# The 128 output rows that a fused retention and MoE kernel computes last, cut as 384 and 128 columns, with the last store issued from ScalarE

## Chip, cores, metric

One core of a Trainium2 chip. The metric is the device time of one execution in microseconds; the "span" is the stretch from the first to the last instruction in a profile, some 1.8 us shorter than that time in the executions of this study that give both. By its time and granted clock (the share of TensorE's full clock that the profiler shows as granted) the record labels each execution fast or slow.

## The reference

Retention (attention with a decay instead of a softmax) over 8 batches, 8 heads, 576 positions and 64 channels, and then a two-layer network with a quick GELU on the 4608 rows:

```python
def _attn_ref(q, k, v):                       # cut
    scores = scale * np.matmul(q, k.transpose(0, 1, 3, 2))
    ret = scores * Dmat[None, :, :, :]        # Dmat: decay, zero above the diagonal
    return np.matmul(ret, v).astype(np.float32)

def _moe_ref(x, w_in, w_out):                 # x: (4608, 512)
    h = x @ w_in                              # w_in: (512, 2048)
    g = h * (1.0 / (1.0 + np.exp(-1.702 * h)))
    return (g @ w_out).astype(np.float32)     # w_out: (2048, 512)
```

Only the last piece of `g @ w_out` to be computed matters below: 128 rows of the output, 512 columns each.

## The kernel before: the parts concerned

The output is made in 36 units of 128 rows. For each unit, `down` multiplies 16 slices of 128 features into one bank of PSUM, the memory that receives TensorE's sums, and `down_out` copies the bank to SBUF, the on-chip working memory (there `osb`), and stores it to the output in DRAM. The helper `op` puts an operation into an engine's stream and derives the waits from what it reads and writes. At the end SyncE waits for the last stores.

```python
def down(c, r, s, b, n0=0, n1=DM):
    for f in range(4 * s, 4 * s + 4):
        op("pe", lambda e, f=f: e.matmul(
            bank[b][:, 0 : n1 - n0], gT[c % 2][:, f, P * r : P * r + P], w_out_sb[:, f, n0:n1],
            start=(f == 0), stop=(f == NF - 1)), ...)

def down_out(c, r, b, n0=0, n1=DM, cp="act"):
    ...
    src, dst = bank[b][:, 0 : n1 - n0], osb[i][:, n0:n1]
    if cp == "act":
        op("act", lambda e: e.activation(dst, src, AF.Copy), ...)
    else:
        op("dve", lambda e: e.tensor_copy(dst, src), ...)
    ...                                        # f issues the store, one DMA per block of rows
    return op("sp", f, reads=[f"osb{i}_{n0}"], ...)

# last chunk of four units, in steady()
if c == NCH - 1:
    for r in (3, 0, 1):
        ...                                    # whole units: 16 matmuls of 512 columns, copy, store
    for n0, b, cp in ((0, "B", "act"), (256, "A", "dve")):
        for s in range(4):
            down(c, 2, s, b, n0, n0 + 256)
        finish_unit(c, 2, b, n0=n0, n1=n0 + 256, cp=cp)
    break
```

So the last unit is already cut in two halves of 256 columns: ScalarE copies the first half while TensorE multiplies the second, and VectorE copies the second.

## Time and profile before

| | before |
|---|---|
| time, median of the first 3 executions | 296.37 us (296.10 to 296.77) |
| span of the profile | 295.1 us |
| TensorE busy | 96% of the span |
| last unit: first matmul to the end of the span | 288.78 to 295.09 us |
| of it, after the last matmul's result | 2.6 us: copy 0.42, store 1.67, closing 0.48, gaps |

The views are read from the whole to the end: first which engine the chain of waits runs through (TensorE), then the timeline of the last 5 us, then the one store that ends last. The prediction shows these lines. "Landing" is the moment when a store's completion is seen, and "closing" is what follows the last landing.

### The profile page before, as it was taken

The numbers are of one execution on the slowest core, as the hardware profiler recorded it, in microseconds if no ns is written. First come the engines' busy times: TensorE is split into PE (matmuls) and PEld (weight loads), VectorE is DVE, ScalarE is ACT, GpSimd is POOL, SyncE is SP. The second block draws the span as 40 slices with busy tenths as digits, with TensorE's granted clock in tenths as the row PEclk, the third lists the DMA queues.
The fourth block names the chain that finished last, engine by engine and source line by source line (L and its number), as shares of the span: only waits on it lengthen the run. The fifth ranks groups of instructions, "written<-read, shape, count | busy, mean of one in ns | idle before, by whom it ended". The sixth has DMA issues, their size and how long they took to land.

```text
span 295.1 us, 8029 instructions
## 1 busy us (share of the span) xinstructions
PE 284.5 (96%) x3620; PEld 142.1 (48%) x3651; DVE 99.6 (34%) x202; ACT 134.0 (45%) x235; POOL 110.1 (37%) x141
## 2 busy tenths in 40 slices
PE   5899999999999999999999999999999999999996
PEld 5567355884533453345434543454344434443344
DVE  5672037534571543034503470237014700410000
ACT  7456433662356225622573246424642365216511
POOL 9999797000970680292039202920080000000000
PEclk9799999999999999999999999999999999999999
DMA  9999999997999999499369925991691050110021
GB/s 169 182 214 205 205 223 252 243 107 176 166 232 117 123 209 207 97 162 197 107 121 144 203 83 131 168 194 63 153 136 66 26 134 2 38 71 38 0 71 71
DMA packets 116786, 40.63 MB, mean 138 GB/s; under 512 B 104080, under 2 KB 109968, under 8 KB 116752
## 3 DMA queue, kind: packets, MB, share of 16 engines
q0 software_dynamic: 79712, 22.82, 67.5%
q1 hardware_dynamic: 37040, 17.31, 23.3%
q8 instruction: 28, 0.46, 0.6%
q14 instruction: 6, 0.05, 0.1%
HBM read 36.70 MB, written 9.44 MB: 156 GB/s over the span
## 4 chain that ended last, share of the span: by engine, by line
PE 95%; DMA 2%; issue 2%; DVE 1%; ACT 0%; SPq 0%
PE psA L582 21%; PE psB L582 20%; PE psA L556 18%; PE psB L556 17%; PE psB L570 4%; PE psA L570 3%; PE psX L481 2%; DMA osb<-in_q_dram 2%; PE psC L497 1%; PE psY L519 1%; PE psX L519 1%; PE psA L674 1%; PE psK L426 1%; PE psE L426 1%; PE psD L497 1%
## 5 line engine op out<-in xcount | busy, mean ns | idle before, releaser
L226 POOL DMA_DIRECT2D kqn<-in_k_dram x39 | 35.2, 913 | 109.0 <-DMA kqT<-kqn 107.3
L582 PE MATMUL psA<-w_out_sb,gT 128*128 128x512 bf16 (+1 forms) x287 | 66.8, 373 | 2.4 <-issue 2.2
L582 PE MATMUL psB<-w_out_sb,gT 128*128 128x512 bf16 (+1 forms) x285 | 63.9, 373 | 0.5 <-issue 0.5
L556 PE MATMUL psB<-xT,w_in_sb 128*128 128x512 bf16 x233 | 61.2, 379 | 0.4
L556 PE MATMUL psA<-xT,w_in_sb 128*128 128x512 bf16 x239 | 61.4, 379 | 0.1
L544 DVE TENSOR_TENSOR xT<-psX,gq 128x512 bf16<-128x512 f32 x16 | 11.1, 691 | 113.4 <-PE psX L519 113.4
L450 ACT ACTIVATE kv<-stm 128x1024 bf16<-128x1024 f32 (+1 forms) x18 | 15.6, 866 | 68.5 <-DVE stm L441 68.5
L582 PEld LDWEIGHTS psB<-w_out_sb,gT 128*128 128x128 bf16 x288 | 27.8, 98 | 31.8 <-ACT gT L561 0.3
L582 PEld LDWEIGHTS psA<-w_out_sb,gT 128*128 128x128 bf16 x304 | 27.8, 98 | 31.7 <-ACT gT L561 2.5
L561 ACT ACTIVATE gT<-psB 128x512 bf16<-128x512 f32 x60 | 35.8, 597 | 15.8 <-PE psB L556 15.7
L561 ACT ACTIVATE gT<-psA 128x512 bf16<-128x512 f32 x60 | 35.8, 597 | 15.6 <-PE psA L556 15.6
L239 POOL DMA_DIRECT2D vn<-in_v_dram x40 | 37.3, 947 | 0.1
L556 PEld LDWEIGHTS psA<-xT,w_in_sb 128*128 128x128 bf16 x240 | 19.1, 97 | 32.6 <-ACT gT L561 16.6
L556 PEld LDWEIGHTS psB<-xT,w_in_sb 128*128 128x128 bf16 x240 | 18.8, 97 | 33.0 <-ACT gT L561 16.3
L226 POOL DMA_DIRECT2D kqn<-in_q_dram x37 | 33.6, 921 | 0.3 <-issue 0.3
L345 DVE TENSOR_TENSOR vp<-vn,vfac 128x512 bf16<-128x512 f32 x36 | 23.2, 684 | 24.0 <-DMA vn<-in_v_dram 24.0
L592 ACT ACTIVATE osb<-psB 128x512 f32<-128x512 f32 (+1 forms) x18 | 10.5, 585 | 21.6 <-PE psB L582 21.6
L592 ACT ACTIVATE osb<-psA 128x512 f32<-128x512 f32 x18 | 10.5, 584 | 15.3 <-PE psA L582 15.3
L506 DVE TENSOR_TENSOR pm<-psC,mask 128x512 bf16<-128x512 f32 (+1 forms) x20 | 12.6, 629 | 8.8 <-PE psD L497 8.7
L506 DVE TENSOR_TENSOR pm<-psD,mask 128x512 bf16<-128x512 f32 (+1 forms) x20 | 12.5, 626 | 0.0
L570 PE MATMUL psB<-xT,w_in_sb 128*128 128x256 bf16 (+1 forms) x104 | 12.5, 265 | 0.0
L441 DVE TENSOR_TENSOR stm<-psE,stm 128x256 f32<-128x256 f32 x28 | 11.9, 424 | 1.2
(86 smaller groups left out, 257.9 us busy)
## 6 DMA issues: line engine op xcount, KB each, us to landing
vn<-in_v_dram POOLq DMA_DIRECT2D x32, 256.0 KB, 5.7
out_dram<-osb SPq DMA_DIRECT2D x31, 256.0 KB, 2.2
kqn<-in_k_dram POOLq DMA_DIRECT2D x31, 128.0 KB, 5.4
kqn<-in_q_dram POOLq DMA_DIRECT2D x31, 128.0 KB, 5.4
w_out_sb<-in_moe_w_out_dram POOLq DMA_DIRECT2D x4, 512.0 KB, 13.4
out_dram<-osb SPq DMA_DIRECT2D x10, 128.0 KB, 2.4
w_in_sb<-in_moe_w_in_dram POOLq DMA_DIRECT2D x8, 128.0 KB, 5.4
w_in_sb<-in_moe_w_in_dram POOLq DMA_DIRECT2D x4, 256.0 KB, 7.5
```

The costliest lines, as they stand in the source:

```text
L226: e.dma_start(kqn[sl][p0 : p0 + n, which, :, :], src[b, :, s0 : s0 + n, :].rearrange("h p d -> p h d"),)
L239: e.dma_start(vn[sl][p0 : p0 + n, :, :], v[b, :, s0 : s0 + n, :].rearrange("h p d -> p h d"))
L345: op(eng, lambda e: e.tensor_tensor(vp[u % NVP].ap(), vn[sl].ap(), vfac[:, ty, :, None].to_broadcast([P, H, DH]), ALU.mult), reads=[f"vn{s ...
L441: op("dve", lambda e: e.tensor_tensor(dst, src, prev, ALU.add), reads=[KB[a], f"stm{(i - 1) % 8}"], writes=[f"stm{i % 8}"])
L450: op("act", lambda e: e.activation(kv[:, i0 % NKV : i0 % NKV + n, :, :], stm[:, i0 % 8 : i0 % 8 + n, :, :], AF.Copy), reads=[f"stm{(i0 + i ...
L506: op("dve", lambda e: e.tensor_tensor(pm[(u0 // 2) % 2][hh][:, c0:c1].rearrange("p (a i) -> p a i", i=64), ps32(SB[hh])[:, c0:c1].rearrang ...
L544: op("dve", lambda e: e.tensor_tensor(xT[ch % 2][:, slice(hh, 4, 2), P * jj : P * jj + 2 * P].rearrange("p g (u t) -> p u g t", u=2), ps32 ...
L556: op("pe", lambda e, a=a: e.matmul(bank[b][:, n0:n1], w_in_sb[:, a, P * f : P * f + P], xT[c % 2][:, a, n0:n1], start=(a == 0), stop=(a == ...
L561: op("act", lambda e: e.activation(gT[c % 2][:, f, n0:n1], bank[b][:, n0:n1], AF.Gelu_apprx_sigmoid), reads=[b], writes=[f"g{c % 2}_{f}_{j ...
L570: op("pe", lambda e, a=a, f=f, i=i: e.matmul(bank[b][:, n * i : n * i + n], w_in_sb[:, a, P * f : P * f + P], xT[c % 2][:, a, P * lo : P * ...
L582: op("pe", lambda e, f=f: e.matmul(bank[b][:, 0 : n1 - n0], gT[c % 2][:, f, P * r : P * r + P], w_out_sb[:, f, n0:n1], start=(f == 0), sto ...
L592: op("act", lambda e: e.activation(dst, src, AF.Copy), reads=[b], writes=[f"osb{i}_{n0}"])
```

## The change

The intent: keep TensorE's work as it is, but leave less to copy and to store after the last matmul. The first piece grows to 384 columns, the last shrinks to 128. The second part of the change issues the last store from ScalarE's queue, so that it need not stand behind the other store in SyncE's.

```diff
-        def down_out(c, r, b, n0=0, n1=DM, cp="act"):
+        def down_out(c, r, b, n0=0, n1=DM, cp="act", eng="sp"):
...
-            return op("sp", f, reads=[f"osb{i}_{n0}"], writes=[f"out{u}_{n0}"],
+            return op(eng, f, reads=[f"osb{i}_{n0}"], writes=[f"out{u}_{n0}"],
...
-                    for n0, b, cp in ((0, "B", "act"), (256, "A", "dve")):
+                    for n0, n1, b, cp in ((0, 384, "B", "act"), (384, 512, "A", "dve")):
                         for s in range(4):
-                            down(c, 2, s, b, n0, n0 + 256)
-                        finish_unit(c, 2, b, n0=n0, n1=n0 + 256, cp=cp)
+                            down(c, 2, s, b, n0, n1)
+                        finish_unit(c, 2, b, n0=n0, n1=n1, cp=cp, eng="sp" if n0 == 0 else "act")
```

## The prediction

> **What bounds the kernel now.** I read three views, from the whole to the last microseconds. First the page: busy time of the engines, and the chain that ended last.
>
> ```profile
> PE 284.5 (96%) x3620; PEld 142.1 (48%) x3651; DVE 99.6 (34%) x202; ACT 134.0 (45%) x235; POOL 110.1 (37%) x141
> ...
> PE 95%; DMA 2%; issue 2%; DVE 1%; ACT 0%; SPq 0%
> ```
>
> TensorE (PE) is busy for 96% of the 295.1 us span and makes up 95% of the chain. No line that the diff touches runs before the last 128-row block, the third unit of the last chunk. So 288.8 us are the same in both kernels, and only the end can move. The timeline from 290.4 us, with start and length ahead of each group:
>
> ```profile
> 290.53 1.91 PE L582 MATMUL psA<-w_out_sb,gT 128*128 128x256 bf16 x16
> 290.73 0.38 ACT L592 ACTIVATE osb<-psB 128x256 f32<-128x256 f32 x1 [1.15 <-PE psB L582]
> 291.14 2.12 SPq L598 DMA_DIRECT2D out_dram<-osb  x2
> 292.48 0.42 DVE L594 COPY osb<-psA 128x256 f32<-128x256 f32 x1 [32.51 <-PE psA L582]
> ```
>
> The second half block is multiplied until 292.44 us (290.53 + 1.91), copied out of PSUM by VectorE (DVE) until 292.90, and stored. That final store, asked for on its own by the window from 292.5 us:
>
> ```profile
> L598 SPq DMA_DIRECT2D out_dram<-osb x1: 332/332/332, 292.9 to 292.9; - x1
> ...
> DMA to landing us min/median/max: 1.7/1.7/1.7
> ```
>
> The reader is to see three steps in a row with nothing beside them: copy 0.42, store 1.7 from its issue at 292.93 to landing at about 294.60, and then 0.49 us of closing handshakes up to 295.09. What the store does in its 1.7 us shows in the sums over three stretches, whose last two columns are DMA share and GB/s:
>
> ```profile
> 293.20:293.76 0.56, 0.00 (x0) 0.00 (x0) 0.00 (x0) 0.00 (x0) 0.00 (x0) 1.00 0.00 0
> 293.76:294.26 0.50, 0.00 (x0) 0.00 (x0) 0.00 (x0) 0.00 (x0) 0.00 (x0) 1.00 0.75 262
> 294.26:294.60 0.34, 0.00 (x0) 0.00 (x0) 0.00 (x0) 0.00 (x0) 0.00 (x0) 1.00 0.00 0
> ```
>
> Of the 1.67 us about 0.83 pass before the first byte, 0.49 move data, and 0.35 pass until the completion is seen. Only the middle part can depend on the size.
>
> **What the Trainium skill says.** "DMA: Bandwidth & Descriptors", section "Issuing engines are not separate DMA queues", states that stores from the scalar and the sync engine end on the same 16 DMA engines, and that issuing from both saves only the sequencer's issue time. The issue here is 0.33 us. The trace can't confirm the ScalarE side: this kernel issues nothing from there. Its section "Anatomy of one DMA — SWDGE (gpsimd) path", written for the other kind of issue, calls most of a DMA's fixed cost a write receipt that doesn't scale with bytes; the 0.35 us of quiet after the last byte agrees in kind, though here it is the smaller part. "TensorE: Matmul & The Clock Gate", section "Back-to-back issue gap", gives a sustained 81 ns for matmuls with 128 columns and calls 56 ns the isolated gap. The trace decides for 56: two runs of sixteen such matmuls with fresh weights, in the timeline around 24.4 us,
>
> ```profile
> 24.65 1.06 PE L570 MATMUL psC<-xT,w_in_sb 128*128 128x128 bf16 x16
> 25.54 1.06 PE L570 MATMUL psB<-xT,w_in_sb 128*128 128x128 bf16 x16
> ```
>
> start 0.89 us apart, 55.6 ns each. "VectorE: DVE Perf Modes", section "Why PSUM operands drop a tier", says that a float32 copy out of PSUM runs at one element per cycle, so its time has a part that falls with the columns; the trace agrees below.
>
> **The change part by part.** The last block is cut as 384 + 128 columns, not 256 + 256, and the small last store is issued by ScalarE.
>
> *Matmuls.* Removed are 2 x 16 of 256 columns, added 16 of 384 and 16 of 128. The steps are 1.75 / 16 = 109 ns at 256 (the two groups of the before start at 288.78 and 290.53), 3.45 / 16 = 216 ns at 512, so 162.5 at 384 by interpolation, and 55.6 at 128. Sum before: 32 x 109 = 3.50 us. Sum after: 16 x 162.5 + 16 x 55.6 = 2.60 + 0.89 = 3.49 us. The last result is due when the last matmul ends: before 290.53 + 1.91 = 292.44. After, the small group starts at 288.78 + 2.60 = 291.38 and takes the 1.06 us of the row above: 292.44. TensorE's end doesn't move. All are on the path, and they cancel.
>
> *Copy of 384 columns, ScalarE.* 383 ns at 256 and 597 at 512, so 490 ns by interpolation. It starts when its matmuls end, 288.78 + 15 x 0.1625 + 0.33 = 291.55, and ends near 292.07, beside the small matmuls. Off the path, and ScalarE is free 0.7 us before it must issue the last store.
>
> *Store of 384 columns, SyncE queue.* Issued near 292.09. Its 192 KB lie between 128 KB (1.7 us) and 256 KB (2.0 us), so it lands in some 1.85 us, at 293.94; data flow from 292.92 to about 293.57. Off the path if the last store lands later.
>
> *Copy of 128 columns, VectorE.* This one is on the path. The copy of 256 took 424 ns; the VectorE rows that read PSUM go from 424 ns (256 columns) to about 685 (512), 1.02 ns for each column. 128 fewer columns save 0.13 us: 0.29 us, end near 292.77.
>
> *Last store, ScalarE queue.* Issue at 292.79 instead of 292.93. From 256 to 128 KB the landing fell by 0.3 us, 2.0 to 1.7, when the row of a partition was halved from 2048 to 1024 bytes. From 128 to 64 KB, rows of 512 bytes, the same slope saves 0.15 us: 1.52 us, if ScalarE issues as fast as SyncE. Its data would flow from 293.62, just after the larger store's end at 293.57, so they don't contend. Landing 294.31 against 294.60, and the 0.49 us of closing stay.
>
> Sum on the path: matmuls 0.00, copy -0.13, store -0.15, together **-0.28 us**, so 0.1% of the time: 296.37 - 0.28 = 296.09, rounded to 296.1.
>
> **The rivals.** *ScalarE is slower to issue.* It has never issued a transfer in this program, and a first one may be cold: SyncE's first two in the trace took 0.46 and 0.57 us against the usual 0.33, so an estimate of +0.13 to +0.25 us on the path. It would eat half to all of the gain: 296.2 to 296.4. I count this as nearly even odds. *The larger store becomes the bound.* It was moved 0.95 us later and made larger. It is predicted to land 0.37 us ahead of the last one, so it takes a misfit of that size, e.g. both streams sharing the DMA engines. Then the end is about 294.3 to 294.6 again and the time stays at 296.1 to 296.4. *Short matmuls are bound by weights.* A weight load shows 98 ns as its length; if that were the step, sixteen would take 1.57 us, +0.67, and the time would be 296.8. The row around 24.65 us speaks clearly against it, since the same 128 x 128 loads kept a step of 55.6 ns. *The 512-byte rows are inefficient.* Were the data part no shorter than at 1024 bytes, 0.15 of the 0.28 us would be lost: 296.2. *A second hardware queue costs something outside the span*: the clock time is about 1.3 us longer than the span (296.37 against 295.1), and I can't see its parts; up to some tenths.
>
> **Range and chances.** All of these lie within -0.3 and +0.7 us, that is -0.1% to +0.2%. The three runs of before alone spread by 0.67 us, and the profiled execution took 296.88, so noise is wider than the effect. From 296.1 I go down and up by that spread, and a little more on the upper side for a cold ScalarE issue: 295.4 to 296.9. A change of 2% is 5.9 us, and the whole stretch from the first edited matmul at 288.78 to the end is 6.3 us, most of it matmuls that stay; a gain of that size is hardly possible, and slower by that would take a stall that nothing in the profile hints at.
>
> **What would show it right or wrong.** Right: the small matmul group starting near 291.4 with length 1.06, the VectorE copy at about 290 ns, the ScalarE issue near 292.8 with 0.33 us, landing 1.5 us later, the 384-column store landing before it, and a span near 294.8. Wrong in a step: an issue on ScalarE of over 0.45 us, or a wait ahead of it; over 1.7 us to landing; a small group longer than 1.1 us; the last wait of SyncE ending with the 384-column store. The total would be wrong if instructions before 288.8 us run differently, or if the chip that times it differs from this one by more than the noise.

## More of the kernel before

For experiments of a quarter of a microsecond I use one more measure, the **tail**: from the start of the first matmul of the last unit to the end of the span, taken from the trace's event times. Everything that the diff edits lies in it.

## The result

The changed kernel took 295.70 us (median of 6, 295.51 to 296.08), the kernel before 296.11 us (median of 6, 295.26 to 296.77). The ratio is 0.9992 with a 95% interval of 0.9973 to 1.0011: the same within 2%, and not to be told from no change at all. (A ratio is the mean time of one kernel's fast executions over that of the other's in the same rounds, so not quite the ratio of these medians.) The time lies within the predicted range, 0.4 us under its centre.

The timeline of the changed kernel from 287.7 us, in the columns start, length, engine and operation:

```profile
287.75 2.76 PE L582 MATMUL psB<-w_out_sb,gT 128*128 128x384 bf16 x16
...
290.35 1.06 PE L582 MATMUL psA<-w_out_sb,gT 128*128 128x128 bf16 x16
290.55 0.49 ACT L592 ACTIVATE osb<-psB 128x384 f32<-128x384 f32 x1 [2.00 <-PE psB L582]
291.44 0.29 DVE L594 COPY osb<-psA 128x128 f32<-128x128 f32 x1 [32.51 <-PE psA L582]
291.77 0.38 ACTq L598 DMA_DIRECT2D out_dram<-osb  x1
```

The groups are those foretold: 16 small matmuls in 1.06 us, a VectorE copy of 0.29 us instead of 0.42, and then an issue that is new in kind, on ScalarE's queue (ACTq), and 0.38 us long. The last store asked for alone:

```profile
L598 ACTq DMA_DIRECT2D out_dram<-osb x1: 378/378/378, 291.8 to 291.8; - x1
...
DMA to landing us min/median/max: 1.6/1.6/1.6
```

Its data, its receipt and the closing, in the sums over stretches (the last two columns are DMA share and GB/s; the first stretch also holds the end of the 384-column store):

```profile
291.77:292.65 0.88, 0.00 (x0) 0.00 (x0) 0.00 (x0) 0.00 (x0) 0.00 (x0) 1.00 0.60 223
292.65:292.99 0.34, 0.00 (x0) 0.00 (x0) 0.00 (x0) 0.00 (x0) 0.00 (x0) 1.00 0.66 193
292.99:293.35 0.36, 0.00 (x0) 0.00 (x0) 0.00 (x0) 0.00 (x0) 0.00 (x0) 1.00 0.00 0
```

The data take 0.34 us instead of 0.49, but start 0.88 us after the issue instead of 0.83.

**Where the time went.** The span fell by 1.25 us, from 295.09 to 293.84, and this is where a hasty reader goes wrong: most of it is not the change. The last unit starts at 288.78 us in the first profile and at 287.75 in the second, 1.03 us earlier, before any edited instruction. In the sums over the first 20 us, where the granted clock stands third from last, the kernel before:

```profile
0.00:10.00 10.00, 6.60 (x134) 4.87 (x137) 6.41 (x23) 6.55 (x21) 9.31 (x19) 0.93 1.11 178
10.00:20.00 10.00, 9.05 (x221) 6.54 (x223) 5.69 (x15) 5.31 (x11) 10.00 (x15) 0.90 1.49 194
```

and the changed kernel:

```profile
0.00:10.00 10.00, 7.19 (x188) 5.60 (x190) 6.48 (x24) 7.37 (x23) 9.31 (x18) 1.00 1.08 177
10.00:20.00 10.00, 9.62 (x216) 6.70 (x205) 6.97 (x17) 5.33 (x11) 10.00 (x16) 1.00 1.49 185
```

The granted clock of TensorE was 0.93 and 0.90 in one execution and full in the other. Whether this belongs to the change is asked in the first experiment. The tail itself went from 6.303 to 6.086 us, **0.217 us less**. By events: matmuls to the start of the last copy 3.695 and 3.693 us (-0.002); the copy 0.424 and 0.291 (-0.133); copy's end to issue 0.027 and 0.032 (+0.005); issue to landing 1.674 and 1.579 (-0.095); landing to end 0.483 and 0.491 (+0.008). The sum is -0.217. Predicted were 0.00, -0.13 and -0.15, together -0.28. One term is off: the store is 0.055 us slower than I had it.

### The profile page after: what moved, and what is told of

It is laid out like the page before. It is cut to its first block, busy times and chain, and to the rows that moved or that the text cites. A ratio compares the mean times of both kernels' runs of the same rounds, so it can differ in the third digit from the quotient of the medians.

```text
span 293.8 us, 8029 instructions
## 1 busy us (share of the span) xinstructions
PE 284.2 (97%) x3620; PEld 140.7 (48%) x3651; DVE 99.0 (34%) x202; ACT 134.0 (46%) x235; POOL 110.4 (38%) x141
## 4 chain that ended last, share of the span: by engine, by line
PE 75%; POOL 16%; DMA 5%; issue 2%; SPq 1%; DVE 0%; POOLq 0%
PE psB L582 18%; PE psA L582 18%; PE psA L556 17%; PE psB L556 16%; POOL kqn L226 8%; DMA vn<-in_v_dram 4%; POOL vn L239 4%; POOL w_in_sb L261 3%; PE psX L481 1%; POOL w_out_sb L268 1%; DMA kqT<-kqn 1%; SPq L391 1%; PE psC L497 1%; PE psX L519 1%; PE psK L426 1%
## 5 line engine op out<-in xcount | busy, mean ns | idle before, releaser
L582 PE MATMUL psA<-w_out_sb,gT 128*128 128x512 bf16 (+1 forms) x287 | 65.9, 370 | 2.4 <-issue 2.2
L582 PE MATMUL psB<-w_out_sb,gT 128*128 128x512 bf16 (+1 forms) x285 | 64.7, 376 | 0.5 <-issue 0.5
L582 PEld LDWEIGHTS psA<-w_out_sb,gT 128*128 128x128 bf16 x304 | 27.2, 98 | 31.7 <-ACT gT L561 2.5
```

The costliest lines, as they stand in the source:

```text
L582: op("pe", lambda e, f=f: e.matmul(bank[b][:, 0 : n1 - n0], gT[c % 2][:, f, P * r : P * r + P], w_out_sb[:, f, n0:n1], start=(f == 0), sto ...
```

## Experiments

The theory that I started with (A): my terms are right, and the missing 0.055 us is the issue on ScalarE, 0.378 us against 0.332. The rivals: the short rows of 512 bytes are slower than the slope of the larger stores said (B); stores on one queue stand behind each other, so that the second queue is needed for the gain (C). A second question is whether ScalarE is slow each time or only the first time. Twelve runs followed, eight new kernels and four repeats, all with correct results. Their tails and store times are collected here first (but for the kernel with all stores on ScalarE, whose profile is of a slow execution); times in us, "landing" and "first data" counted from the issue, "tail" to the end of the span. Where a kernel has two profiles, both are given.

| kernel | columns | last copy, last issue | copy | issue | first data | landing | tail |
|---|---|---|---|---|---|---|---|
| before | 256, 256 | VectorE, SyncE | 0.424, 0.425 | 0.332, 0.332 | 0.836, 0.834 | 1.674, 1.682 | 6.303, 6.312 |
| changed | 384, 128 | VectorE, ScalarE | 0.291, 0.292 | 0.378, 0.368 | 0.885, 0.873 | 1.579, 1.571 | 6.086, 6.087 |
| size alone | 384, 128 | VectorE, SyncE | 0.292, 0.291 | 0.332, 0.333 | 0.831, 0.832 | 1.525, 1.525 | 6.022, 6.037 |
| queue alone | 256, 256 | VectorE, ScalarE | 0.425 | 0.367 | 0.873 | 1.719 | 6.362 |
| ScalarE used before | 384, 128 | VectorE, ScalarE | 0.292 | 0.339 | 0.847 | 1.545 | 6.061 |
| copy by ScalarE | 384, 128 | ScalarE, SyncE | 0.277, 0.277 | 0.332, 0.332 | 0.835, 0.836 | 1.519, 1.521 | 6.014, 6.016 |
| 64 columns last | 448, 64 | VectorE, SyncE | 0.224 | 0.431 | 1.024 | 1.766 | 6.437 |
| 64, other queue | 448, 64 | VectorE, ScalarE | 0.225 | 0.369 | 1.249 | 1.981 | 6.430 |
| 96 columns last | 416, 96 | ScalarE, SyncE | 0.250 | 0.394 | 0.961 | 1.703 | 6.170 |

The second values come from repeats, which show the scatter: 0.01 us, or 0.015 where landing to end took 0.498 instead of 0.483 us, as it did in some profiles of several kernels.

### The kernel before against itself

No edit. Expected:

> The kernel before, unchanged, against itself. From the first matmul of the last row block to the end of the span: 6.30 us again, within 0.02 us, if this stretch is a repeatable measure. The start of that block (288.78 us in the first profile) may move by up to 1 us: theory A says that the 1.03 us by which the changed kernel reached it earlier (287.75) is the lead-in's varying clock and not the change, so this profile may fall anywhere between 287.5 and 289. The rival, that the second queue shortens the part before, expects 288.8 again within 0.1 us. Ratio of times 1.000 within its interval, some 0.2% wide to each side.

Measured: the ratio of the kernel before to itself is 0.9992, interval 0.9956 to 1.0028 (medians 295.67 and 296.55 us, 6 and 11 executions on one chip). The change's own ratio was 0.9992. A clock comparison at this scatter gives an unchanged kernel the same "gain". The tail came again at 6.312 us, and the last unit started at 287.65 us, where the first profile had 288.78. In its sums over the lead-in the clock was full:

```profile
0.00:10.00 10.00, 7.44 (x189) 5.75 (x192) 6.79 (x25) 7.43 (x23) 9.31 (x19) 1.00 1.11 177
10.00:20.00 10.00, 9.48 (x204) 6.50 (x203) 6.68 (x16) 5.33 (x11) 10.00 (x16) 1.00 1.48 186
```

So the same code reaches the last unit 1.13 us earlier: a difference of the size of the 1.03 us comes without the change. Across the profiles of all kernels but one (that with all stores on ScalarE, below), this start lies between 287.40 and 290.40 us. The three with a dipped clock in the lead-in are among the late ones (288.78, 288.67 and 289.82); but two with a full clock started at 290.40 and 289.72, so theory A, which put it down to the clock, named only a part. The traces show another: how soon the first inputs land. In the first profile the chain that ended last begins with the first load of q, 4.83 us long, and TensorE waits 1.9 us for the tile made from it; in the repeat the load took 3.8 us and the wait 0.6:

```profile
1.25 4.83 DMA osb<-in_q_dram
...
PE psB L361 <- DVE kqn L257: 1.9, 1, 1.9
...
PE psB L361 <- DVE kqn L257: 0.6, 1, 0.6
```

(The first line gives start and length on the chain, the others the wait in us, how often, and the longest; the first two lines are of the first profile, the last is of the repeat.) A first load near the head of the chain also marks three other late profiles: 5.12 us for q where the unit started at 290.40, 5.40 us for k at 288.67, 6.43 us for v at 289.82. By the start of the first output copy the profiles already lie between 37.4 and 40.3 us. In the one of 289.72 TensorE waits 1.3 us at line 570 of the kernel for something that the profile doesn't name. Why the loads differ stays open.

### The changed kernel again

No edit to it. Expected:

> The changed kernel once more. Block start to end: 6.09 us within 0.02, with ScalarE's issue at 378 ns and the store landing 1.58 us after it. Ratio of times: 6.09 against 6.30 is -0.21 us, so 0.9993; not to be told from 1 by the clock alone.

Measured: ratio 0.9996 (0.9970 to 1.0021), tail 6.087 us, issue 0.368, landing 1.571. The tail repeats to 0.001 us; the gain of the tail over the kernel before is 0.22 us in both pairs of profiles.

### The size alone

```diff
-finish_unit(c, 2, b, n0=n0, n1=n1, cp=cp, eng="sp" if n0 == 0 else "act")
+finish_unit(c, 2, b, n0=n0, n1=n1, cp=cp, eng="sp")
```

> 384 and 128 columns, both stores issued by SyncE. Theory A (my missing 0.06 us is the slower issue on ScalarE): issue 0.332 us, first data 0.835 us after its start, landing 1.53 us after it, block start to end 6.03 to 6.04 us, 0.05 less than the changed kernel. Theory B (rows of 512 bytes are what is slower than the slope said, whoever issues): landing 1.58, stretch 6.08. Theory C (a second store on the same queue queues up behind the first): landing over 1.6, stretch over 6.1.

Measured: ratio 0.9988 (0.9964 to 1.0012), tail 6.022 us. The last store asked for alone:

```profile
L598 SPq DMA_DIRECT2D out_dram<-osb x1: 332/332/332, 291.8 to 291.8; - x1
...
DMA to landing us min/median/max: 1.5/1.5/1.5
```

Landing came 1.525 us after issue; I had predicted 1.52 by the slope, on the condition that ScalarE issues as fast as SyncE. With SyncE issuing, the whole predicted gain is there: the middle of 6.022 and 6.037 against the middle of 6.303 and 6.312 is -0.278 us. Theory B falls (the rows of 512 bytes keep to the slope), and so does C at this cut: SyncE's issue of the larger store ends 0.36 us before the last one is due.

The repeat of this kernel was expected thus:

> Repeat of the kernel with the size alone, for the scatter of the stretch: 6.02 us within 0.02, issue 0.332 us, first data 0.83 us after it.

It gave a tail of 6.037 us with the same landing, 1.525, so the 0.015 us are in the closing. It ran on another chip than the first; the tail hardly depends on that.

### The queue alone

```diff
-for n0, n1, b, cp in ((0, 384, "B", "act"), (384, 512, "A", "dve")):
+for n0, n1, b, cp in ((0, 256, "B", "act"), (256, 512, "A", "dve")):
```

> 256 and 256 columns as before, the last store issued by ScalarE. Theory A: issue 0.378 us, landing 1.72 us instead of 1.67, stretch 6.35 us, 0.05 longer than before. Theory B: landing 1.67 and stretch 6.30 as before. If the queue were the part of the change that helps: under 6.25.

Measured: tail 6.362 us, **0.054 longer** than the middle of the kernel before. Issue 0.367 us, first data 0.873, landing 1.719:

```profile
L598 ACTq DMA_DIRECT2D out_dram<-osb x1: 367/367/367, 291.7 to 291.7; - x1
```

The ratio by the clock was 0.9984 (0.9958 to 1.0011), the lowest of the four kernels of these rounds, for the one whose tail is the longest. That is noise again, and shows why the trace and not the clock must decide here. The four corners now add up: size alone -0.278, queue alone +0.054, sum -0.224; both together, the changed kernel, -0.221. At these cuts the two parts of the change add up within the scatter, and the second works against the first.

### ScalarE used for stores before

Is ScalarE's issue slow each time, or only as its first? In this kernel the two whole units ahead of the last one are also stored from ScalarE.

```diff
-                        finish_unit(c, r, b)
+                        finish_unit(c, r, b, eng="sp" if r == 3 else "act")
```

> As the changed kernel, and the two whole-row stores ahead of the last block are issued by ScalarE too, so that the last store is ScalarE's third. If ScalarE is slow only the first time (cold): first issue 0.38 us or more, last 0.33 us, landing 1.53, stretch 6.04 us. If it is slower each time: all three 0.37 to 0.39 us, first data 0.88 us after issue, stretch 6.09 us.

Measured, in the timeline, all three issues of ScalarE:

```profile
286.04 0.38 ACTq L598 DMA_DIRECT2D out_dram<-osb  x1
...
289.50 0.34 ACTq L598 DMA_DIRECT2D out_dram<-osb  x1
...
292.69 0.34 ACTq L598 DMA_DIRECT2D out_dram<-osb  x1
```

The first took 0.375 us, the later ones 0.339. Landing came after 1.545 us and the tail was 6.061. So of the 0.05 us that ScalarE costs, about 0.03 (0.367 to 0.378 against 0.339) is a first-use cost, and the rest, 0.01 to 0.02 us in issue and first data, is there each time.

### All output stores from ScalarE

```diff
-        def down_out(c, r, b, n0=0, n1=DM, cp="act", eng="sp"):
+        def down_out(c, r, b, n0=0, n1=DM, cp="act", eng="act"):
...
-finish_unit(c, 2, b, n0=n0, n1=n1, cp=cp, eng="sp" if n0 == 0 else "act")
+finish_unit(c, 2, b, n0=n0, n1=n1, cp=cp, eng="act")
```

> All 41 output stores issued by ScalarE, the columns as in the changed kernel. If slower each time by a constant: nearly all issues of undisturbed stores 0.37 to 0.39 us against SyncE's 0.33. ScalarE then spends about 41 x 0.4 = 16 us on issues beside its 134 us of work; TensorE waits for its GELU in pairs of banks, so if a wait for a store's issue holds up a copy or a GELU, the time grows by up to some us; if not, the time is that of the changed kernel within 0.3 us. My guess: 0 to +1 us.

On the issues it agrees with the last experiment: the first took 0.378 us, the commonest values are 0.338 and 0.339 (27 of 41). The median is no comparison with SyncE's 0.332: SyncE's own 41 issues in the kernel before have a median of 0.338 too, while 0.332 and 0.333 are its commonest values (19 of 41). The last store, from a ScalarE long in use, landed 1.548 us after its issue, near the 1.545 above.

```profile
L598 ACTq DMA_DIRECT2D out_dram<-osb x41: 332/338/615, 38.3 to 300.7; - x41
```

On the time my guess of 0 to +1 us was wrong: the three fast executions lie at 1.0191 of the kernel before (1.0145 to 1.0236), so some 6 us more. At the 2% line the record's verdict is "unclear", since the interval lies on both sides of it; that it is slower is clear of noise. The profile is of an execution labelled slow, so I read only its form. TensorE stalls once, in the waits between 90 and 120 us:

```profile
PE psC L497 <- DMA kqT<-kqn: 3.5, 1, 3.5
```

and the sums over that stretch show what follows:

```profile
98.00:102.00 4.00, 0.59 (x64) 0.59 (x64) 0.60 (x1) 0.00 (x0) 0.00 (x0) 1.00 1.15 115
102.00:106.00 4.00, 4.00 (x26) 1.53 (x13) 3.78 (x9) 0.00 (x0) 0.11 (x1) 0.57 0.31 70
```

A transposed tile (a DMA from SyncE's queue) is late by 3.5 us; after the pause the granted clock is 0.57 for a 4 us stretch. The transposes' median from issue to landing is 7.5 us here and 2.8 in the repeat of the changed kernel; other transfers land later too, the 256 KB stores after 5.7 us against 2.6 and the 256 KB loads of v after 9.7 against 6.0. Without the stores in SyncE's queue the four transposes of this stretch begin at 80.99 us instead of 83.55, but the fourth is issued only at 100.88 instead of 94.09: between 60 and 125 us SyncE waits 39.1 us in eight waits for loads of q, and in the repeat for none of them. So the order of the transfers changed and loads came late. Why they did, and whether the fast executions lose their time in the same place, stays open.

### Smaller last pieces

```diff
-for n0, n1, b, cp in ((0, 384, "B", "act"), (384, 512, "A", "dve")):
+for n0, n1, b, cp in ((0, 448, "B", "act"), (448, 512, "A", "dve")):
```

First with both stores on SyncE:

> 448 and 64 columns, both on SyncE. If a matmul's step is columns / 2.4 plus 2 ns down to 64 columns (29 ns), the sum of both groups stays at 3.5 us and the stretch falls to about 5.93 us. If the step can't fall below the 55 ns or so that 128 columns take, because each brings a weight load of 128 columns: 16 x 189 + 16 x 55 = 3.90 us, 0.41 more than with 384 and 128; copy 64 ns shorter and landing up to 80 ns shorter; stretch 6.30 us, no better than before.

Neither branch was right. Sixteen matmuls of 64 columns stepped by 29 ns, so no floor at 55 ns: the matmuls ended when they did before. The copy fell to 0.224 us. Yet the tail is 6.437 us, longer than before the change. The store's data started 1.024 us after its issue and landing took 1.766. The issue itself came late: the small copy ended 3.92 us after the start of the unit, but SyncE was issuing the larger store until 4.13 and began at 4.17. That seemed a case for the second queue, so the same cut ran with the last issue on ScalarE:

> 448 and 64 columns with the last store issued by ScalarE; with both on SyncE the stretch was 6.44 us, since SyncE was busy issuing the larger store until 0.21 us after the small copy's end, and the small store's data then came 1.02 us after its issue, behind the larger one's. Theory A' (a second queue pays where the first is busy): ScalarE issues 0.03 us after the copy's end (3.95 us from the block's start, against 4.17), the small store lands at about 5.6 to 5.8 us instead of 5.94, the larger store becomes the last to land or nearly so (5.77), and the stretch falls to 6.27 to 6.35 us. Rival (all transfers share the engines and the order of the data stays the same, so the queue is of no use): 6.42 us or more.

In its timeline ScalarE issues while SyncE is still busy:

```profile
291.10 0.23 DVE L594 COPY osb<-psA 128x64 f32<-128x64 f32 x1 [32.51 <-PE psA L582]
291.20 0.33 SPq L598 DMA_DIRECT2D out_dram<-osb  x1
291.35 0.37 ACTq L598 DMA_DIRECT2D out_dram<-osb  x1
```

The issue started 0.22 us earlier (3.95 us into the unit), and nothing came of it: tail 6.430 us. My theory A' fell and the rival held. The first data of the small store came at 5.199 us into the unit, against 5.197 with both on SyncE: the same moment, whichever queue issued it and whenever. The sums show what the engines did until then:

```profile
291.35:292.03 0.68, 0.00 (x0) 0.00 (x0) 0.00 (x0) 0.00 (x0) 0.00 (x0) 1.00 0.00 0
292.03:292.60 0.57, 0.00 (x0) 0.00 (x0) 0.00 (x0) 0.00 (x0) 0.00 (x0) 1.00 0.98 380
292.60:292.95 0.35, 0.00 (x0) 0.00 (x0) 0.00 (x0) 0.00 (x0) 0.00 (x0) 1.00 0.55 130
```

From 292.03 to 292.60 they are 98% busy with the larger store; 292.60 is 5.20 us into the unit. With 8 rows of 1792 bytes for each of the 16 DMA engines at about 0.074 us each, the first engine is through after some 0.59 us, an estimate from the median length of this store's data packets in the trace, and only then takes up the small store. The events agree: each store ends with sixteen packets of 4 bytes, and in this trace the larger store's first one starts at 5.193 us into the unit, 6 ns before the small store's first data. The same at 416 and 96 columns:

> 416 and 96 columns, both stores on SyncE, last copy by ScalarE (as in the best version with another cut). If copy and store of the last piece alone count: 27 ns less for the copy and up to 40 ns less to landing, stretch 5.95 us. If the larger store's data, due until about 5.07 us from the block's start, hold up the small store's (first due at 4.8): 6.0 us or more, so that 384 and 128 is already the best cut.

Measured: tail 6.170 us, first data at 4.93 us into the unit; the first engine is through with the larger store's 8 rows at about 4.94 (4.388 + 8 x 0.069, again from the packets). With 384 and 128 the same estimate gives 4.67 us, and the small store's data aren't due before 4.85: it doesn't have to wait. Of the four cuts tried, 256, 384, 416 and 448, 384 has the shortest tail, and it is the largest of them whose two stores don't meet. Cuts in between were not tried.

### The last copy by ScalarE

```diff
-for n0, n1, b, cp in ((0, 384, "B", "act"), (384, 512, "A", "dve")):
+for n0, n1, b, cp in ((0, 384, "B", "act"), (384, 512, "A", "act")):
...
-finish_unit(c, 2, b, n0=n0, n1=n1, cp=cp, eng="sp" if n0 == 0 else "act")
+finish_unit(c, 2, b, n0=n0, n1=n1, cp=cp, eng="sp")
```

> 384 and 128 columns, both stores on SyncE, and the last copy by ScalarE, which is idle by then. ScalarE's copies of 256 and 384 columns took 383 and 491 ns, so 276 ns at 128 by the same slope, against VectorE's 291. If copy and issue simply add: 0.015 us less than with the size alone, stretch 6.02 us. If SyncE sees ScalarE's semaphore later than VectorE's: no gain, 6.04 us or more. Ratio of times about 0.999.

Measured: the copy took 0.277 us, the tail was 6.014 us, the shortest. By the clock the ratio is 0.9998 (0.9977 to 1.0018). The repeat:

> Repeat of the best version: stretch 6.01 us within 0.02; whether its 0.008 us less than with the size alone is more than scatter is open, the copies' 0.277 against 0.292 us should come again.

gave 6.016 us. Up to the landing, where the closing's 0.015 us of scatter don't enter, this version has 5.515 and 5.517 us, the size alone 5.539 and 5.538: 0.02 us less, beyond scatter, with the copy's 0.015 in it. Against the kernel before the tail is 0.29 us shorter. That is the best version that I found, and it is the same as all others by the clock.

Not tried: both engines copying 64 columns each of the last piece. What it would bring is open.

## Why the prediction was right, and where not

- **TensorE's end doesn't move: right.** The second group started 2.600 us after the first (predicted 2.60), the last copy 3.693 us after the start of the first (3.695 before). The rival that weight loads bound the small matmuls fell; even 64 columns stepped by 29 ns.
- **Copy -0.13 us: right**, 0.424 to 0.291.
- **Store -0.15 us: the term that was mis-sized.** It was stated "if ScalarE issues as fast as SyncE", and ScalarE didn't. With SyncE the term measures -0.15 (landing 1.525), with ScalarE -0.095 to -0.11. The rival that I gave nearly even odds, a cold first issue on ScalarE, is what happened, but at 0.03 to 0.05 us instead of the 0.13 to 0.25 that I took from SyncE's first two transfers. Those two loads, issued in the first 1.3 us of the program, were no measure for a first store at its end.
- **The larger store doesn't become the bound: right.** It landed 0.395 us ahead of the last (predicted 0.37), and its data ended 0.11 us before the other's began (predicted 0.05).
- **"288.8 us are the same in both kernels": wrong as a statement on one execution.** The instructions are the same (one edited line, the store's in `down_out`, does run for every unit, but with `eng="sp"` it issues as before), but their time isn't; it moved by 1.03 us between the two first profiles, nearly five times the effect, with the first load of q landing 1.0 us sooner and the clock full in the second. The predicted span of 294.8 and the absolute starts failed by that much (measured 293.8), and the time fell 0.4 us under the centre for no reason that the change gives.
- **Two slips in its working, which change no conclusion.** The "1.3 us" by which the clock time is longer than the span compares a median of other executions with the profiled one, which itself took 296.88 us: the difference is 1.8. And the upper end of "-0.3 and +0.7" counts from 296.1, not from the kernel before: its worst rival, 296.8, is +0.4 on 296.37.
- **Within 2%: right**, and the sum on the path, -0.28, measures -0.22 for the change as a whole and -0.28 for its first part alone.

## What to carry to other kernels

Behind the last matmul, what shrinks with the size is small (here about 1 ns for each column of the copy, and 0.15 us for half of a 128 KB store), so cut the last piece unevenly, but only as far as the larger store is through when the smaller one's data are due. A second queue for the last store cost 0.05 us here, and where the first was still busy issuing (448 and 64 columns) it brought nothing either, because the DMA engines were full; measure each part of such a change alone. When an effect is a thousandth of the time, compare the stretch that was edited, event by event, in repeated traces, and run the kernel before against itself first.

## What the Trainium skill lacked or had wrong

- "TensorE: Matmul & The Clock Gate", section "Back-to-back issue gap": it gives 81 ns (128 columns) and 131 ns (512) for sustained pairs of weight load and matmul, and calls its formula of columns / 2.4 + 2.5 ns the isolated gap. In sustained pairs the runs show the formula: 29 ns at 64 columns, 56 at 128, 163 at 384, 189 at 448, 216 at 512.
- "DMA: Bandwidth & Descriptors", section "Issuing engines are not separate DMA queues": that a second issuing engine saves only issue time is borne out (issued 0.22 us sooner, the tail changed by 0.007 us), but it lacks the first use. ScalarE's first issue took 0.367 to 0.378 us in six profiles, later ones mostly 0.338 or 0.339, SyncE's most often 0.332. It also says that transfers interleave; here a small store's data waited until an engine was through with its 8 rows of the larger store, at 5.20 us into the last unit from either queue. The same page's section "Queues, rings and completion order" would explain that (an engine drains a whole packet of some 9 to 17 descriptors before it turns to another ring, and by that count 8 rows would fit in one); no run here shows where such a packet ends.
- The same page, section "Anatomy of one DMA — SWDGE (gpsimd) path": it puts most of the fixed cost on the write receipt. For these stores from SyncE and ScalarE, 0.83 to 0.89 us pass ahead of the first byte and about 0.35 us after the last, where no other store is in the way (0.43 to 0.47 in the cuts whose stores meet); the receipt is the smaller part. A time of the receipt on this path is lacking.
- No page that I read says how far the landing of one and the same load varies from execution to execution: the first load of q landed 3.4 to 5.1 us after its issue. The start of the last unit, with the same work ahead of it, lay between 287.40 and 290.40 us.
